# Loading the last head pair's output weights behind all of V, in two DMAs, and projecting head by head

## The chip, the cores and the metric

The kernel runs on one core of a Trainium2 chip. The metric is device time in microseconds (us). This program has one core, so its time is that core's.

## The reference, cut to what matters

One decode step: one token `x` of width 448, 16 query heads of size 256, 8 key/value heads over a cache of 65,536 positions, then a projection with `wo` (4096 x 448), mixed with a small MLP by a gate.

```python
q = (x @ wq).reshape(B, Sq, 16, 256).transpose(0, 2, 1, 3)
scores = einsum("bhqd,bhkd->bhqk", q, repeat(k_cache, 2, 1)) * 256 ** -0.5
o = einsum("bhqk,bhkd->bhqd", softmax(scores), repeat(v_cache, 2, 1))
a = o.transpose(0, 2, 1, 3).reshape(B, Sq, 4096) @ wo
...                                     # b: layer norm, MLP over the token axis
return g * a + (1 - g) * b              # g = sigmoid(sum(x * gate_w))
```

K and V are 268 MB each and are read once. Everything else is small. The heads come in pairs that share one K/V head: 8 pairs, each with a `wo` share of 512 x 448 values, 448 KB.

## The kernel before

The SyncE queue issues all big loads in one order. A pair has four blocks, each of 8 MB of K and 8 MB of V (`NP` = 32 blocks, `PPH` = 4 blocks per pair). The last V is cut into four parts, of 96, 16, 12 and 4 tiles (6144, 1024, 768 and 256 KB). Each pair's `wo` is issued behind the V of the pair's first block.

```python
for j in range(NP):
    last = j == NP - 1
    ...                                   # wait, then load K of block j (last: two halves)
    load(vbuf, A_v_cache, j, 0, NFIRST if last else NV, 0, sem_v)
    if last:
        for (n0, n1), sem in zip(pieces, sem_vp):
            load(vbuf, A_v_cache, j, n0, n1, 0, sem)
    if j % PPH == 0:
        g = j // PPH
        if g >= 1:
            eng.wait_ge(s_proj, g)        # the projection before has read wo_sb
        ...                               # load wo of pair g into wo_sb
```

After the last block TensorE does this. `values` has already added the first 112 V tiles into `acc`, and VectorE copies that sum to `accs`. (`spin(1)` is one matmul whose result nobody uses.)

```python
def tail():
    pe.wait_ge(s_cp, H)                              # accs is there
    by_d(sps[:, 0, 0:2 * REP])                       # early sum, transposed
    late_values(NLATE, NV).then_inc(s_late, 1)       # last 16 V tiles, 32 matmuls
    spin(1)
    pe.wait_ge(sem_wo, 16 * H)
    pe.wait_ge(s_oTn, H)                             # VectorE: normalised o
    project([dj * REP + hh for hh in range(REP) for dj in range(2)])   # 16 matmuls
```

VectorE then computes `out_g` (gate and sum), and SyncE stores it.

The softmax here doesn't subtract the row's maximum and nothing guards it: scores larger than these inputs give would overflow.

## Time and profile before

| | before |
|---|---|
| median of 6 runs | 1267.35 us (1267.10 to 1267.81) |
| span of the profiled run | 1265.2 us |
| share of the 16 DMA engines that the load queue holds | 99.6% |
| TensorE, ScalarE, VectorE busy | 72%, 42%, 33% |
| last V part landed; `out_g` started | 1261.60; 1262.77 us |

From the page of the kernel before: the busy line, the load queue (packets, MB, share of 16 engines) and the chain that ended last.

```profile
PE 913.4 (72%) x17110; PEld 864.6 (68%) x17110; DVE 420.5 (33%) x755; ACT 537.4 (42%) x786; POOL 0.9 (0%) x7
...
q1 hardware_dynamic: 11512, 544.22, 99.6%
...
DMA 70%; PE 29%; issue 1%; DVE 0%; SPq 0%; ACT 0%; ACTq 0%
```

One queue fills the DMA engines for the whole span. So the time is the bytes, plus a short start, plus what is left to do after the last byte.

The DMA issues of the kernel before (size, then median us from issue to landing), and the SyncE timeline near the end (start, duration, what):

```profile
vbuf<-in_A_v_cache_dram SPq DMA_DIRECT2D x1, 6144.0 KB, 25.7
wo_sb<-in_A_wo_dram SPq DMA_DIRECT2D x8, 448.0 KB, 27.6
...
vbuf<-in_A_v_cache_dram SPq DMA_DIRECT2D x1, 256.0 KB, 29.1
```

```profile
1117.53 0.39 SPq L261 DMA_DIRECT2D wo_sb<-in_A_wo_dram  x1
...
1230.90 2.00 SPq L229 DMA_DIRECT2D vbuf<-in_A_v_cache_dram  x4
```

The V and `wo` loads shown here take 26 to 29 us to land although 256 KB need far less (the last part landed 0.64 us after the part ahead of it): each waits behind the loads issued ahead of it. The last `wo` was issued at 1117.53 and is used at 1262.35, so it lies in SBUF unused for over 115 us.

The end of the kernel before, from its timeline (start, duration, engine, line, operation, out<-in, count; in brackets the idle time before and what ended it):

```profile
1256.67 3.23 PE L350 MATMUL acc<-vbuf,pT 128*2 128x256 bf16 x112 [0.73 <-DMA vbuf<-in_A_v_cache_dram]
1259.95 0.46 DVE L564 COPY accs<-acc 128x288 f32<-128x288 f32 x1 [7.24 <-PE acc L350]
...
1261.00 1.00 PE L371 MATMUL sps<-pT,vbuf 128*128 128x2 bf16 x32
...
1262.03 0.16 DVE L575 TENSOR_TENSOR oTn<-sps,rden 128x4 bf16<-128x4 f32 x1 [1.11 <-PE sps L371]
...
1262.35 0.37 PE L397 MATMUL prj<-wo_sb,oTn 128*1 128x112 bf16 x16
1262.77 0.33 DVE L621 SCALAR_TENSOR_TENSOR out_g<-prj,bcast,run_g 128x112 bf16<-128x112 f32 x1 [0.57 <-PE prj L397]
1263.13 0.65 SPq L264 DMA_DIRECT2D out_dram<-out_g  x1
```

The trace also records 16 landings for each of these DMAs, read here as one for each engine's share. The last of the 16 came at 1256.63, 1259.10, 1260.96 and 1261.60 us for the four parts of V. From the last landing to the start of `out_g` pass 1262.77 - 1261.60 = 1.17 us, in which no byte is loaded.

### The profile page before, as it was taken

What the parts mean: (1) busy time and instruction counts of PE and PEld (TensorE: products, weight loads), DVE (VectorE), ACT (ScalarE), POOL (GpSimd) and SP (SyncE); (2) the same over time, 40 slices, a digit from 0 to 9 for tenths busy, and PEclk for the clock granted to TensorE, in tenths of its full rate; (3) what the DMA queues carried; (4) which work ended last, traced back from release to release, by engine and by line L of the source; (5) the groups of instructions that cost most, each with busy time, mean ns of one, the idle gap of its engine ahead of it and who ended that gap; (6) DMA issues with size and microseconds to landing.
All of it is one profiled execution on the core that took longest, in us unless ns stands there. A gap on an engine that the chain in (4) does not pass through costs nothing.

```text
span 1265.2 us, 38823 instructions
## 1 busy us (share of the span) xinstructions
PE 913.4 (72%) x17110; PEld 864.6 (68%) x17110; DVE 420.5 (33%) x755; ACT 537.4 (42%) x786; POOL 0.9 (0%) x7
## 2 busy tenths in 40 slices
PE   3866678766778667786676876768867678675688
PEld 2766668766677666686666876657766578665687
DVE  2333334423344233343222332223322233332233
ACT  1443335533355333454333553335533345433455
POOL 0000000000000000000000000000000000000000
PEclk9878789878798788888788888788888798787999
DMA  9999999999999999999999999999999999999998
GB/s 412 425 436 433 431 433 433 435 433 435 431 433 433 435 431 437 431 431 433 437 431 433 435 431 433 437 431 433 433 433 433 429 437 435 433 433 431 431 428 352
DMA packets 11613, 544.39 MB, mean 430 GB/s; under 512 B 1360, under 2 KB 1618, under 8 KB 2898
## 3 DMA queue, kind: packets, MB, share of 16 engines
q1 hardware_dynamic: 11512, 544.22, 99.6%
q8 instruction: 8, 0.13, 0.0%
q10 hardware_dynamic: 90, 0.01, 0.0%
q14 instruction: 3, 0.02, 0.0%
HBM read 544.22 MB, written 0.00 MB: 430 GB/s over the span
## 4 chain that ended last, share of the span: by engine, by line
DMA 70%; PE 29%; issue 1%; DVE 0%; SPq 0%; ACT 0%; ACTq 0%
DMA kring<-in_A_k_cache_dram 68%; PE kst L295 24%; PE sps L315 4%; DMA vbuf<-in_A_v_cache_dram 2%; PE acc L350 1%; PE sps L371 0%; PE sps L378 0%; DVE accs L564 0%; SPq L226 0%; PE prj L397 0%; SPq L224 0%; PE acc L339 0%; DVE out_g L621 0%; PE kst L331 0%; ACT pT L646 0%
## 5 line engine op out<-in xcount | busy, mean ns | idle before, releaser
L295 PE MATMUL kst<-ident,kring 128*128 128x128 f32 x4096 | 560.5, 298 | 311.3 <-DMA kring<-in_A_k_cache_dram 300.5
L657 ACT ACTIVATE ktT<-kst 128x1024 bf16<-128x1024 bf16 x512 | 499.5, 1021 | 668.6 <-PE kst L295 667.8
L295 PEld LDWEIGHTS kst<-ident,kring 128*128 128x128 f32 x4096 | 510.7, 155 | 321.2 <-issue 318.5
L559 DVE COPY ktT<-kst 128x1024 bf16<-128x1024 bf16 x512 | 354.2, 692 | 766.5 <-PE kst L295 743.3
L315 PEld LDWEIGHTS sps<-qcur,ktT 128*128 128x128 bf16 x8192 | 237.8, 96 | 4.6 <-issue 2.1
L315 PE MATMUL sps<-qcur,ktT 128*128 128x2 bf16 x8192 | 236.6, 163 | 1.7 <-issue 1.7
L350 PE MATMUL acc<-vbuf,pT 128*2 128x256 bf16 x4080 | 140.3, 305 | 2.6 <-issue 1.8
L350 PEld LDWEIGHTS acc<-vbuf,pT 128*2 128x2 bf16 x4080 | 104.9, 93 | 29.7 <-issue 2.3
L646 ACT ACTIVATE pT<-sps 128x32 f32 x256 | 52.2, 204 | 16.7 <-PE sps L315 16.7
L339 PE MATMUL acc<-pT,ones_sq 128*128 128x32 bf16 x256 | 11.7, 178 | 12.2 <-ACT pT L646 12.2
L339 PEld LDWEIGHTS acc<-pT,ones_sq 128*128 128x128 bf16 x256 | 8.6, 96 | 15.1 <-ACT pT L646 14.9
L663 ACT ACTIVATE z_b<-z_b 128x448 bf16<-128x448 bf16 x14 | 8.1, 576 | 20.6 <-DVE z_b L546 20.6
L564 DVE COPY accs<-acc 128x288 f32<-128x288 f32 x8 | 3.7, 458 | 38.4 <-PE acc L350 38.4
L386 PEld LDWEIGHTS acc<-sel,accs 128*64 128x64 f32 x112 | 10.8, 214 | 0.9
L386 PE MATMUL acc<-sel,accs 128*64 128x1 f32 x112 | 11.4, 261 | 0.0
L421 PE MATMUL acc<-vbuf 42*128 42x42 bf16 x1 | 0.2, 214 | 8.3 <-DMA b_b<-in_B_b_dram 8.3
L540 DVE TENSOR_TENSOR z_b<-wtmp,u_b 128x448 bf16<-128x448 bf16 x14 | 5.5, 393 | 1.0
L538 DVE TENSOR_TENSOR wtmp<-u_b 128x448 bf16<-128x448 bf16 x14 | 5.5, 392 | 1.1
L544 DVE TENSOR_TENSOR z_b<-u_b,wtmp 128x448 bf16<-128x448 bf16 x14 | 5.5, 392 | 1.0
L552 DVE TENSOR_TENSOR gu<-wtmp,z_b 128x448 bf16<-128x448 bf16 x14 | 5.5, 392 | 1.0
L421 PEld LDWEIGHTS acc<-vbuf 42*128 42x128 bf16 x1 | 0.1, 98 | 8.3 <-DMA b_b<-in_B_b_dram 8.3
L550 DVE TENSOR_SCALAR z_b<-z_b 128x448 bf16<-128x448 bf16 x14 | 3.9, 277 | 5.5 <-ACT z_b L663 5.5
(85 smaller groups left out, 79.1 us busy)
## 6 DMA issues: line engine op xcount, KB each, us to landing
kring<-in_A_k_cache_dram SPq DMA_DIRECT2D x4, 4096.0 KB, 24.2
vbuf<-in_A_v_cache_dram SPq DMA_DIRECT2D x1, 6144.0 KB, 25.7
wo_sb<-in_A_wo_dram SPq DMA_DIRECT2D x8, 448.0 KB, 27.6
vbuf<-in_A_wq_dram SPq DMA_DIRECT2D x1, 3072.0 KB, 10.1
vbuf<-in_A_v_cache_dram SPq DMA_DIRECT2D x1, 1024.0 KB, 27.5
vbuf<-in_A_v_cache_dram SPq DMA_DIRECT2D x1, 768.0 KB, 29.0
vbuf<-in_A_wq_dram SPq DMA_DIRECT2D x1, 512.0 KB, 10.9
vbuf<-in_A_v_cache_dram SPq DMA_DIRECT2D x31, 30.0
```

What stands on the lines that cost most here:

```text
L295: ins = pe.transpose(kst[:, b, i * P:(i + 1) * P], kring_f[:, at + NT * (k % DC) + 4 * b + i, :], ident[:, :])
L315: ins = pe.matmul(sps[:, par, 2 * nt:2 * nt + 2], ktT[:, par, b, ntl * DH + dj:(ntl + 1) * DH:2], qcur[:, dj, :], start=(dj == 0), stop=(d ...
L339: pe.matmul(acc[:, DENC:SELC], ones_sq[:, :], pT[:, r, :], start=False, stop=(r == BODY - 1), skip_group_check=True)
L350: ins = pe.matmul(acc[o:o + REP, 0:DH], pT[:, r, 2 * nt:2 * nt + 2], vbuf[:, n, :], start=False, stop=False, skip_group_check=True)
L386: ins = pe.matmul(dst[hh * HP:(hh + 1) * HP, i:i + 1], accs[:, i:DH:2 * REP], sel[:, hh:hh + 1], start=False, stop=True, skip_group_check= ...
L538: vec.tensor_tensor(W, U, U, op=ALU.mult)
L540: vec.tensor_tensor(Z, W, U, op=ALU.mult)
L544: vec.tensor_tensor(Z, U, W, op=ALU.add)
L559: vec.tensor_copy(ktT[:, k % KTB, b, :], kst_b[:, b, :]).then_inc(sem_ev[b], 1)
L646: act.activation(pT[:, bass.ds(p0 + k % DC, 1), :].rearrange("p o n -> p (o n)"), sps[:, k % 2, 0:2 * NT], AF.Exp, scale=scale).then_inc(s ...
L657: act.activation(ktT[:, k % KTB, b, :], kst_b[:, b, :], AF.Copy).then_inc(sem_ev[b], 1)
L663: act.activation(z_b[:, :], z_b[:, :], AF.Tanh).then_inc(s_tanh, 1)
```

## The change

The intent: the stream's last place should belong to the load that has the least work behind it. V's last part has late values, normalising and the whole projection behind it. `wo` has only the projection, and half of that if it comes in two halves.

```diff
+        sem_wl = [new_sem("sem_wl%d" % h) for h in range(REP)]
...
-                if j % PPH == 0:
-                    g = j // PPH
+                g, m = divmod(j, PPH)
+                if m == 0 and g < H - 1:
...                                       (pairs 0 to 6 load as before; the last pair's branch is gone)
+            eng.wait_ge(s_proj, H - 1)
+            for h in range(REP):
+                w = A_wo[(HQ - REP + h) * DH:(HQ - REP + h + 1) * DH, :]
+                eng.dma_start(wo_sb[:, h, :], w.rearrange("(p j) n -> p (j n)", j=2)).then_inc(sem_wl[h], 16)
...
-            def project(cols):
-                for i, j in enumerate(cols):
+            def project(cols, i0=0):
+                for i, j in enumerate(cols, i0):
...
-                pe.wait_ge(sem_wo, 16 * H)
                 pe.wait_ge(s_oTn, H)
-                project([dj * REP + hh for hh in range(REP) for dj in range(2)])
+                for h in range(REP):
+                    pe.wait_ge(sem_wl[h], 16)
+                    ins = project([dj * REP + h for dj in range(2)], 2 * h)
+                ins.then_inc(s_proj, 1)
```

Bytes and matmuls are the same. There is one DMA more and one wait more.

More of the change, by code (lines that the diff above doesn't have):

```diff
@@ L257, in _ @@
                     w = A_wo[g * REP * DH:(g + 1) * REP * DH, :]
-                    if g < H - 1:
-                        eng.dma_start(wo_rows, w.rearrange("(p i) n -> p (i n)", i=2 * REP)).then_inc(sem_wo, 16)
-                    else:
-                        eng.dma_start(wo_sb[:, :, :], w.rearrange("(h p j) n -> p h (j n)", h=REP, j=2)
-                                      ).then_inc(sem_wo, 16)
+                    eng.dma_start(wo_rows, w.rearrange("(p i) n -> p (i n)", i=2 * REP)).then_inc(sem_wo, 16)
+            eng.wait_ge(s_proj, H - 1)
+            for h in range(REP):
+                w = A_wo[(HQ - REP + h) * DH:(HQ - REP + h + 1) * DH, :]
+                eng.dma_start(wo_sb[:, h, :], w.rearrange("(p j) n -> p (j n)", j=2)).then_inc(sem_wl[h], 16)
             eng.wait_ge(s_fin, 1)
@@ L399, in project @@
                                         start=False, stop=True, skip_group_check=True)
-                ins.then_inc(s_proj, 1)
+                return ins
             def tail():
@@ L466, in _ @@
                     pe.wait_ge(s_oTn, g + 1)
-                    project(range(2 * REP))
+                    project(range(2 * REP)).then_inc(s_proj, 1)
         @block.vector
```

## The prediction

> **What bounds the kernel.** The DMA stream. The page's queue part gives q1 a 99.6% share of the 16 engines for 544 MB at 430 GB/s; TensorE is busy 72%, VectorE 33%, ScalarE 42%; the chain of waits is 70% DMA. Inside the stream, fewer or better-ordered compute instructions are worth nothing. Only bytes count there, and what runs after the last byte.
>
> **The end, before (timeline from 1235 us and landings of the trace).** K's second half of the last block lands at 1242.1, V's 6144 KB part at 1256.63, the pieces of 1024, 768 and 256 KB at 1259.10, 1260.96 and 1261.60. Then: 32 late-value matmuls 1261.00 to 1262.00, VectorE's oTn 1262.03 (0.16 us), 16 projection matmuls 1262.31 to 1262.72, out_g 1262.77 (0.33 us), output DMA issued at 1263.13, span end 1265.2. So about 1.1 us of work lies between the last landing and out_g, and the DMA engines stand idle there.
>
> **What the change does.** It takes no byte away. The last pair's wo (448 KB) is now issued at 1117.5, during V of block 28, and needed only at 1262; its 1792-byte packets take 75 ns each, 16 per engine, so 1.2 us of every engine. Moved behind V, it lets all of K and V from block 29 on land 1.2 us earlier, and lands itself where V's last piece landed: about 1261.6 (one more semaphore packet of 9 ns on each engine). [...]
>
> **Critical path after.** V's main part lands at 1255.4, TensorE is ready for it (its keys hang on K, also 1.2 us earlier). Early values end near 1258.7, accs is copied by 1259.2, late values run 1259.8 to about 1260.75 (last piece lands 1260.4), oTn is ready by 1261.0. wo's first head lands near 1261.0, the second near 1261.6: 0.6 us of slack for the attention chain. The first head's 8 matmuls are hidden. After the last landing stay 0.05 us of wake-up, 8 matmuls (about 0.3 us with fill, by the present 16 in 0.41 including weight loads) and out_g, which then starts near 1262.0 instead of 1262.77. Gain about 0.75 us of 1267.4, that is 0.06%. Two waits instead of one on TensorE and two DMA issues instead of one on the SP queue (0.33 to 0.39 us each, 28 us before they land) cost nothing.
>
> **Prediction: 1266.7 us, range 1265.8 to 1267.5. Faster by over 2%: 0.005; within 2%: 0.99; slower by over 2%: 0.005.** The gain is about as large as the spread of the three runs (1267.1 to 1267.81).
>
> **What would show each step.** Right: mean GB/s and bytes unchanged; V's last piece to landing about 1.2 us earlier; the late-value matmuls start near 1259.8; before the projection's second half an idle of 0.3 to 0.6 us, released by DMA of wo_sb; out_g about 0.75 us earlier; the output tail unchanged at about 2.4 us. The last wo landing within 0.1 us of 1261.6.
>
> **What would make it wrong.** The late DMAs start a new pause in the queue, or their short packets at the end land later than bytes alone say (then a loss of up to 0.5 us); the 1.2 us given back at block 29 is not kept because a K load there waits for TensorE (then no gain, or wo arrives 1.2 us after V: +0.4 us); the attention chain doesn't move up and oTn still ends last; drift between chips or runs of a microsecond, larger than the effect.

## The result, and the profile after

| | before | after |
|---|---|---|
| median (range) of 6 runs each | 1267.35 (1267.10 to 1267.81) | 1266.47 (1266.35 to 1266.54) |
| span of the profiled run | 1265.2 | 1264.3 |
| V's last part landed | 1261.60 | 1260.35 |
| last load landed | 1261.60 (V) | 1261.53 (`wo`, second head) |
| from there to `out_g` | 1.17 | 0.36 |

A ratio here is the mean time of one kernel's runs over that of the other's of the same rounds, so it is not quite the ratio of the medians quoted. It is 0.9992, 95% interval 0.9980 to 1.0005. The interval includes 1, but the slowest of the six runs after (1266.54) is faster than the fastest of the six before (1267.10). The changed kernel was run in three more series of five beside the kernel before, and there too no run of one overlaps the other (means 0.80, 0.77 and 0.68 us apart). So there is a gain, and it is about 0.06%.

The page after, the same lines:

```profile
PE 916.7 (73%) x17110; PEld 864.9 (68%) x17110; DVE 420.4 (33%) x755; ACT 536.7 (42%) x786; POOL 0.9 (0%) x7
...
q1 hardware_dynamic: 11528, 544.22, 99.7%
...
DMA 71%; PE 28%; issue 1%; SPq 0%; DVE 0%; ACT 0%; ACTq 0%
```

The 16 packets more are the extra DMA's semaphore packets, of 4 bytes and 9 ns in the median. The issues and the SyncE timeline after:

```profile
vbuf<-in_A_v_cache_dram SPq DMA_DIRECT2D x1, 6144.0 KB, 24.5
...
wo_sb<-in_A_wo_dram SPq DMA_DIRECT2D x2, 224.0 KB, 28.1
vbuf<-in_A_v_cache_dram SPq DMA_DIRECT2D x1, 256.0 KB, 27.9
```

```profile
1230.85 2.00 SPq L230 DMA_DIRECT2D vbuf<-in_A_v_cache_dram  x4
1232.90 0.90 SPq L264 DMA_DIRECT2D wo_sb<-in_A_wo_dram  x2
```

V is issued at the same time as before and lands 1.2 us sooner after its issue (24.5 in place of 25.7): there are 448 KB less ahead of it. The end after:

```profile
1255.39 3.23 PE L352 MATMUL acc<-vbuf,pT 128*2 128x256 bf16 x112 [0.72 <-DMA vbuf<-in_A_v_cache_dram]
1258.67 0.46 DVE L568 COPY accs<-acc 128x288 f32<-128x288 f32 x1 [7.22 <-PE acc L352]
...
1259.77 0.98 PE L373 MATMUL sps<-pT,vbuf 128*128 128x2 bf16 x32
...
1260.79 0.16 DVE L579 TENSOR_TENSOR oTn<-sps,rden 128x4 bf16<-128x4 f32 x1 [1.15 <-PE sps L373]
...
1261.08 0.27 PE L399 MATMUL prj<-wo_sb,oTn 128*1 128x112 bf16 x8
...
1261.57 0.27 PE L399 MATMUL prj<-wo_sb,oTn 128*1 128x112 bf16 x8 [0.22 <-DMA wo_sb<-in_A_wo_dram]
1261.89 0.33 DVE L625 SCALAR_TENSOR_TENSOR out_g<-prj,bcast,run_g 128x112 bf16<-128x112 f32 x1 [0.94 <-PE prj L399]
1262.25 0.65 SPq L266 DMA_DIRECT2D out_dram<-out_g  x1
```

Every line of the attention end has the same duration as before (3.23, 0.46, 1.00 or 0.98, 0.16 us) and starts 1.2 to 1.3 us earlier. New is the wait in front of the second eight matmuls, which DMA ends. (The step from `oTn` to the projection changed by little; see early_by_head.) The gain in this pair of traces is `out_g` at 1261.89 in place of 1262.77, 0.88 us. Of these, 1.17 - 0.36 = 0.81 us are work that no longer lies behind the last landing, and 0.07 us are that the last landing itself came earlier. That small part can't be told from chance: the experiments show the last landing of one program vary by 0.3 us.

### The profile page after: what moved, and what is told of

Same layout as the page of the kernel before. It is cut to its first block, busy times and chain, and to the rows that moved or that the text cites. A ratio compares the mean times of both kernels' runs of the same rounds, so it can differ in the third digit from the quotient of the medians.

```text
span 1264.3 us, 38824 instructions
## 1 busy us (share of the span) xinstructions
PE 916.7 (73%) x17110; PEld 864.9 (68%) x17110; DVE 420.4 (33%) x755; ACT 536.7 (42%) x786; POOL 0.9 (0%) x7
## 3 DMA queue, kind: packets, MB, share of 16 engines
q1 hardware_dynamic: 11528, 544.22, 99.7%
## 4 chain that ended last, share of the span: by engine, by line
DMA 71%; PE 28%; issue 1%; SPq 0%; DVE 0%; ACT 0%; ACTq 0%
DMA kring<-in_A_k_cache_dram 68%; PE kst L297 24%; PE sps L317 4%; DMA wo_sb<-in_A_wo_dram 2%; PE acc L352 0%; SPq L230 0%; SPq L264 0%; SPq L227 0%; SPq L225 0%; PE acc L341 0%; DVE out_g L625 0%; PE prj L399 0%; ACT pT L650 0%; ACTq L650 0%
## 5 line engine op out<-in xcount | busy, mean ns | idle before, releaser
L352 PE MATMUL acc<-vbuf,pT 128*2 128x256 bf16 x4080 | 147.6, 315 | 2.2 <-issue 1.5
L352 PEld LDWEIGHTS acc<-vbuf,pT 128*2 128x2 bf16 x4080 | 109.3, 96 | 32.3 <-issue 2.0
L399 PE MATMUL prj<-wo_sb,oTn 128*1 128x112 bf16 x128 | 3.6, 240 | 3.2 <-DVE oTn L591 2.8
## 6 DMA issues: line engine op xcount, KB each, us to landing
vbuf<-in_A_v_cache_dram SPq DMA_DIRECT2D x1, 6144.0 KB, 24.5
```

Of the source, the lines that this page charges most:

```text
L352: ins = pe.matmul(acc[o:o + REP, 0:DH], pT[:, r, 2 * nt:2 * nt + 2], vbuf[:, n, :], start=False, stop=False, skip_group_check=True)
```

## The experiments

Theory A: the stream is full, so its end stays where it is whatever the order. The change trades V for `wo` in the last place, and the gain is the work that thereby no longer lies behind the last landing. Rival B: taking `wo`, and the queue's wait on a projection, out of block 28 makes the stream itself shorter. Rival C: the projection head by head is what shortens the end.

There were twelve experiments, four in a series on one chip, each of five runs beside nine of the kernel before. "Against before" is the difference of the means of the runs of the same series. Landings are the last of a DMA's shares unless a mean over the 16 engines is named. Edits are against the changed kernel.

| run | median us | mean against before | last landing of V; of the last load | `out_g` |
|---|---|---|---|---|
| same_after (series 1) | 1266.69 | -0.80 | 1260.36; 1261.54 | 1261.90 |
| late_one_dma (1) | 1266.70 | -0.71 | 1260.38; 1261.52 | 1262.14 |
| early_by_head (1) | 1267.39 | -0.11 | 1261.28; 1261.28 | 1262.35 |
| between_k_v (1) | 1267.19 | +0.10 | 1261.56; 1261.56 | 1262.63 |
| same_after2 (series 2) | 1266.46 | -0.77 | 1260.28; 1261.43 | 1261.80 |
| no_wo (2) | 1266.14 | -1.21 | 1260.63; 1260.63 | 1261.70 |
| dummy_load (2) | 1267.86 | +0.44 | 1261.77; 1262.92 | 1263.29 |
| eight_rings (2) | 1269.60 | +2.13 | 1260.86; 1264.67 | 1265.12 |
| same_after3 (series 3) | 1266.57 | -0.68 | 1260.57; 1261.73 | 1262.18 |
| late_one_dma2 (3) | 1267.02 | -0.35 | 1260.34; 1261.48 | 1262.21 |
| eight_dmas (3) | 1268.03 | +0.70 | 1260.85; 1263.32 | 1263.77 |
| eleven_rings (3) | 1267.24 | +0.02 | 1261.07; 1262.48 | 1262.85 |

### same_after, same_after2, same_after3: the changed kernel again

No edit.

> The changed kernel once more, as the yardstick of this series. Theory A (order at the end: wo takes the last place in the stream, so that only half a projection is left after the last landing) and all rivals: 1266.5 us, about 0.9 us under the kernel before; V's last piece lands near 1260.35, wo's second head near 1261.5, out_g starts near 1261.9.

> The changed kernel again, for comparison on the chip of this series: 1266.5 us.

> The changed kernel again, for comparison on the chip of this series: 1266.5 us, 0.8 us under the kernel before.

All three came as expected. They also show how far one trace may be trusted: the last landing is 1261.54, 1261.43 and 1261.73 for the same program. The 16 engines end at different times, and that spread differs from run to run (2.0, 1.8 and 2.3 us here). The mean over the 16 engines is steadier: 1260.45, 1260.58, 1260.63. So below 0.3 us a single last landing proves nothing.

### late_one_dma and late_one_dma2: behind V, but in one piece

```diff
-            for h in range(REP):
-                w = A_wo[(HQ - REP + h) * DH:(HQ - REP + h + 1) * DH, :]
-                eng.dma_start(wo_sb[:, h, :], w.rearrange("(p j) n -> p (j n)", j=2)).then_inc(sem_wl[h], 16)
+            eng.dma_start(wo_sb[:, :, :], A_wo[(HQ - REP) * DH:HQ * DH, :].rearrange("(h p j) n -> p h (j n)", h=REP, j=2)
+                          ).then_inc(sem_wl[0], 16)
...
+                pe.wait_ge(sem_wl[0], 16)
                 for h in range(REP):
-                    pe.wait_ge(sem_wl[h], 16)
```

> wo behind all of V, but in one DMA and with one wait, so that all 16 projection matmuls come after the last landing. Theory A: the place of wo makes most of the gain and the split only the difference of 16 to 8 matmuls, about 0.1 us: 1266.6 us, still 0.8 us under the kernel before. Rival C (the projection head by head is what shortens the end): no gain, 1267.3 us.

> wo behind V in one DMA once more, because in the first series its trace had out_g 0.24 us later than the changed kernel's and its runs only 0.01 us in the median. If the trace is right: 0.2 us slower than the changed kernel in the runs too, still 0.6 us under the kernel before. If the split is worth nothing: no difference again.

The place without the split gives 0.71 us of 0.80 in the first series, but only 0.35 of 0.68 in the second, where 0.6 was expected. Rival C forecast no gain here, and has fallen as the main cause. The split is worth 0.08 us in the means of the first series and 0.34 in the second. In the traces, from last landing to `out_g`, it takes 0.62 and 0.73 us, against 0.36, 0.37 and 0.45 with the split. That is more than the 0.1 us that the matmuls alone account for. The timeline of late_one_dma2 and, below it, its windows (PE, PEld, DVE, ACT and POOL busy with counts, granted clock, DMA):

```profile
1261.62 0.54 PE L398 MATMUL prj<-wo_sb,oTn 128*1 128x112 bf16 x16 [0.64 <-DMA wo_sb<-in_A_wo_dram]
1262.21 0.34 DVE L624 SCALAR_TENSOR_TENSOR out_g<-prj,bcast,run_g 128x112 bf16<-128x112 f32 x1 [1.27 <-PE prj L398]
```

```profile
1261.40:1261.70 0.30, 0.08 (x8) 0.11 (x12) 0.00 (x0) 0.00 (x0) 0.00 (x0) 0.50 0.00 0
1261.70:1262.00 0.30, 0.30 (x16) 0.20 (x14) 0.00 (x0) 0.00 (x0) 0.00 (x0) 0.50 0.00 0
```

The 16 matmuls took 0.54 us where the kernel before needed 0.37, and the granted clock was 0.50. In the profiled run after, the clock was 1.00 through these windows. The clock differs from run to run here: same_after3 had 0.50 too from 1261.4 on, with both halves of the projection slowed (274 ns for a matmul in the median, 210 in the run after). So part of what the split seems to gain is the clock of the particular run. In late_one_dma the clock fell during the projection (0.68 over 1261.70 to 1262.00), so no trace shows the single DMA at full clock. With two series that differ by a factor of four, the worth of the split stays between 0.1 and 0.3 us and is not settled further.

### early_by_head: in two DMAs and head by head, but loaded early

```diff
                     eng.dma_start(wo_rows, w.rearrange("(p i) n -> p (i n)", i=2 * REP)).then_inc(sem_wo, 16)
+                if m == 0 and g == H - 1:
+                    ...                  # the lines cut below
-
-            eng.wait_ge(s_proj, H - 1)
-            for h in range(REP):
-                ...                       (the two DMAs)
```

> Two DMAs, two semaphores and the projection head by head, but wo loaded in block 28 where the kernel before has it. Theory A: nothing gained, 1267.35 us (within 0.2 us), V's last piece back at 1261.6, out_g at 1262.8. Rival C: most of the gain stays, about 1266.5 us.

The mean is 0.11 us under the kernel before, within the spread of the runs. The trace's last V landing lies at 1261.28, earlier than in the kernel before by the spread of the engines (mean 1260.45 against 1260.53), and `out_g` follows it by 1.07 us, near the 1.17 of the kernel before and far from the 0.36 of the changed one. Splitting gains at most 0.1 us where `wo` has long been there. This is the second half of the case against rival C. The 0.1 us may be real: in the three traces with the changed tail and no late `wo` (this one, between_k_v and no_wo) the projection starts 0.06 us after `oTn` is done and `out_g` 1.07 us after the last landing, against 0.16 and 1.17 us in the one trace before. Which edit of the tail would do this was not tested by itself.

### between_k_v: taken out of block 28, but ahead of the last V

```diff
+                if last:
+                    ...                  # wait on s_proj and the two DMAs, as below
                 load(vbuf, A_v_cache, j, 0, NFIRST if last else NV, 0, sem_v)
...
-            eng.wait_ge(s_proj, H - 1)
-            for h in range(REP):
-                ...                       (the two DMAs)
```

> wo taken out of block 28 and loaded at the end, but in front of the last block's V and behind its K. Theory A: V's last piece lands at 1261.6 again and the whole attention end comes after it, so 1267.35 us (within 0.2 us) although the last K lands 1.2 us earlier. Rival B (taking wo and its wait on the projection out of the queue in block 28 makes the stream itself shorter): about 1266.5 us.

This is the run against rival B: block 28 is free of `wo` and of the wait, and little or nothing is gained. Four of five runs lie at 1267.14 to 1267.21, 0.3 us under the median before (0.1 of it may be that of early_by_head); one of 1269.12 lifts the mean. Rival B's 1266.5 us are not there. The last K lands at 1240.86 as in the changed kernel, so the stream does move up from block 28 on. But V comes behind `wo` and lands at 1261.56. Timeline:

```profile
1256.62 3.23 PE L352 MATMUL acc<-vbuf,pT 128*2 128x256 bf16 x112 [1.91 <-DMA vbuf<-in_A_v_cache_dram]
...
1261.99 0.16 DVE L579 TENSOR_TENSOR oTn<-sps,rden 128x4 bf16<-128x4 f32 x1 [1.11 <-PE sps L373]
1262.21 0.37 PE L399 MATMUL prj<-wo_sb,oTn 128*1 128x112 bf16 x16
```

TensorE now stands 1.91 us before V in place of 0.73: the 1.2 us that the last K gained turned into a wait for V.

### no_wo: the bound

```diff
-            for h in range(REP):
-                ...                       (the two DMAs)
...
-                    pe.wait_ge(sem_wl[h], 16)
```

> The last pair's wo is not loaded at all and the projection uses what lies there (a wrong result on purpose): what the change could gain at most. Theory A: the stream ends 1.2 us earlier (16 packets of 75 ns per engine) and the old end with all its work moves up whole: 1266.1 us, 1.2 us under the kernel before; V's last piece lands near 1260.35, oTn at 1260.8, out_g near 1261.55. Then the change has taken 0.8 to 0.9 of 1.2 us. Rival B (the stream doesn't move up by its bytes): less than 0.5 us under the kernel before.

The mean gains 1.21 us, as expected: taken out at the end, 448 KB are worth 1.2 us. The changed kernel, which loads these bytes, gets 0.77 us in the same series. So moving the load takes about two thirds of what dropping it would (0.8 to 0.9 of 1.2 us were expected), and at most 0.44 us are left to any other arrangement of this load. The result is wrong on purpose, and yet the comparison with the reference passed. Presumably the attention of this problem, averaged over 65,536 positions, is too small for the tolerance; that was not measured. So that comparison says nothing about the changed projection; it was verified by reading only: `i` still runs 0 to 3 over `oTn` columns 0, 2, 1, 3.

### dummy_load: the same bytes once more where they were

```diff
+        spare = sb([P, 2 * REP * DM], bf16, "spare")
...
+                if m == 0 and g == H - 1:
+                    eng.wait_ge(s_proj, g)
+                    eng.dma_start(spare[:, :], A_wo[0:REP * DH, :].rearrange("(p i) n -> p (i n)", i=2 * REP)
+                                  ).then_inc(sem_sp, 16)
```

> The changed kernel, with 448 KB that nobody uses loaded in block 28, where wo was, with the same wait on the projection. Theory A: the stream is full, every byte counts wherever it stands: 8 packets of 144 ns per engine, 1.15 us over the changed kernel, 1267.65 us, all landings at the end 1.15 us later. Rival B (a load of this size in mid-stream hides in a pause): the changed kernel's time, 1266.5 us.

It lost 0.44 + 0.77 = 1.21 us against the changed kernel in the means. The last landing came 1.49 us later, but by the mean over the engines 1261.73 - 1260.58 = 1.15 us, the number expected. The spread of this run was 2.3 us against 1.8 and made up the rest. There is no pause at block 28 in which a load would hide, and no gain from the place as such: rival B's second chance is gone.

### eight_rings, eight_dmas, eleven_rings: can the spread of the engines be used?

The spread is in place early: K's first landings lie 1.6 us apart in the profiled run after, the second's 2.0, and it stays at 2.0 to the end. If the early engines could take more of the last load, up to half of that might be gained (an estimate: in the profiled run after, the last landing lies 0.9 us behind the mean of the 16). Where V's parts and each head of `wo` left 16 landings, the 16 DMAs of 8 partitions left 144 records, 16 x 8 + 16, and 8 packets each beside the data (the load queue has 11640 packets in eight_rings, 11528 after: 112 more, 16 x 8 - 16); two DMAs of 88 and 40 left 23 records, 11 + 10 + 2. The expectations read 8, 11 and 10 as the engines in use, the same 8 for all sixteen DMAs and the 10 among the 11, so that five get none of the load in eleven_rings. That was the author's estimate. Which engines were taken, no trace shows.

```diff
-                w = ...
-                eng.dma_start(...)
+                w = A_wo[(HQ - REP + h) * DH:(HQ - REP + h + 1) * DH, :].rearrange("(p j) n -> p (j n)", j=2)
+                at = 0
+                for np_ in ((P,) if h == 0 else SIZES):
+                    eng.dma_start(wo_sb[at:at + np_, h, :], w[at:at + np_, :]).then_inc(sem_wl[h], 16)
+                    at += np_
```

SIZES is `(8,) * 16` in eight_rings (which writes the same with a step), `(16,) * 8` in eight_dmas and `(88, 40)` in eleven_rings. TensorE waits for the full count, 16 for each DMA.

> The 16 shares of each DMA land spread over 2.0 us (wo's second head from 1259.60 to 1261.53), the spread is as wide all the way, and the wait ends with the latest. Here the second head is loaded in 16 DMAs of 8 partitions[...]. If those 8 are the early ones: wo lands near 1261.0, about 0.4 us gained over the changed kernel (1266.1 us). If they are the late ones: 0.6 us later, 1267.1 us. If mixed: in between, 0.3 to 0.6 us lost.

> The second head in 8 DMAs of 16 partitions[...]. It tells apart why loading on 8 engines lost 3.1 us. If the landings of small DMAs one behind the other cost about 0.2 us each on an engine (the spacing of the last landings there): wo lands about 1.0 us later, 1267.5 us. If the loss came from the uneven load of the engines: under 0.2 us lost, 1266.6 us.

> The second head in two DMAs of 88 and 40 partitions[...]. If the latest engines are among the five: wo lands up to 0.3 us earlier than in the changed kernel. If the latest is among the ten: 4 packets of 75 ns more and one more semaphore packet, 0.3 to 0.5 us later, 1266.9 us.

eight_rings was a miss: 2.9 us slower than the changed kernel of its series, far outside all three expectations. The data were late by only a part of that. The last data packet ended at 1262.46, 1.48 us later than in same_after2 (1260.98), but the last landing was recorded at 1264.67, 2.21 us after it, where same_after2 has 0.45. So of the 3.24 us by which the last landing was later, 1.48 are later data and 1.76 a longer way from last packet to last landing. The last landings lie 0.20 us apart (1264.08, 1264.27, 1264.47, 1264.67). Issuing was not the cause:

```profile
1233.16 19.17 SPq L266 DMA_DIRECT2D wo_sb<-in_A_wo_dram  x17
```

All were issued by 1252.3, and the first packet of this `wo` came at 1257.9. (The last packets took 0.19 us each in place of 0.08; why is open.) So eight_dmas was made: half as many DMAs, of 16 partitions each. That they use all 16 engines was the author's estimate, not shown. It was 1.39 us slower than the changed kernel (expected: 1.0). The data ended at 1261.65, 0.43 us later than in same_after3 (1261.22). The last landing came at 1263.32, 1.67 us after that (0.51 in same_after3), and the last ones again lie 0.19 to 0.20 us apart, here behind packets of 0.08 us. So the last landing was 1.59 us later with the load cut into eight, and sixteen DMAs, in eight_rings, cost about twice as much in device time (2.9 against 1.39 us). That speaks for the number of small DMAs as the main cost; what the number of engines costs was not measured apart.

eleven_rings has only two DMAs and was 0.71 us slower than the changed kernel (expected: 0.3 to 0.5). Its last landing is 0.75 us later. `wo`'s packets of 1792 bytes took 93 ns in the median against 76. Why they were slower was not tested and stays open. In all three runs V's last part, which is issued ahead of `wo`, landed later too: at 1260.86 in eight_rings (1260.28 in same_after2), at 1260.85 and 1261.07 in eight_dmas and eleven_rings (1260.57 in same_after3). This is not explained either. No run here made use of the spread. None beat the changed kernel with a right result.

## Why the prediction was right

- **What bounds it.** "Only bytes count there, and what runs after the last byte": dummy_load and no_wo cost and gave 1.2 us for 448 KB, and between_k_v gained no more than 0.3 us from a freer block 28.
- **The stream's end.** "lands itself where V's last piece landed: about 1261.6": 1261.53 in the trace after; by the mean over the engines 1260.62 against 1260.53. The bytes moved, and the end did not. The loads at the end landed in the order of their issue: V's last part 1260.35, `wo` 1260.95 and 1261.53. The trace doesn't name the engine of a landing, so an order on each engine is not shown; the pattern fits it, as the 16 landings of one load follow those of the load before at the same distances to within 0.1 us (`wo`'s first head 0.55 to 0.62 us after V's last part).
- **The attention chain.** V's main part was forecast at 1255.4 (1255.34), late values from 1259.8 (1259.77), oTn by 1261.0 (1260.95). This chain had to move up whole, or the change would have gained nothing. It did, because its first link is a wait for DMA: 0.73 us before, 0.72 after.
- **After the last landing.** The prediction left 0.05 us of wake-up, 8 matmuls in about 0.3, then `out_g` near 1262.0. Measured 0.04, about 0.3, and 1261.89. The wait for the second half was forecast at 0.3 to 0.6 us; the weight loads waited 0.38, within it, and the matmuls 0.22, below it.
- **The size.** Forecast 1266.7, measured 1266.47, within the range. The gain was put at about 0.75 us. The medians give 0.88 and the repeated series 0.68 to 0.80. The one-trace excess is the 0.07 us earlier last landing, smaller than the spread between runs of one program.
- **What it did not see.** It took the clock of TensorE as given. In one of the four profiled runs of the changed kernel (same_after3) the clock was 0.50 for the projection (1.00 in the run after), and the step from landing to `out_g` took 0.45 in place of 0.36 us.

## What to carry to other kernels

Where loads fill the whole span, the order of the last loads is free and decides what lies exposed behind the last byte: put last the load with the least work behind it, even if it could have been there long before. The gain is the difference of the work behind the two candidates (here 0.8 us), bounded by the time of the moved bytes (1.2 us), so read both from the trace before taking the trouble. Do not cut the last load into many small DMAs: here eight of 28 KB in place of one of 224 KB landed 1.6 us later, about 0.2 us for each.

## What the runs leave open

- How closely the landings of small DMAs can follow one another, and why. The semaphore packets took 9 ns each in the median. In eight_dmas the last landings lie 0.19 to 0.20 us apart although a data packet takes 80 ns, and eight small DMAs ended 1.6 us later than one of the same bytes. The traces do not show what part of a landing takes this time.
- Small DMAs cost much here although the queue was full and nothing waited for the issue: with 28 KB each in eight_dmas, 1.6 us more for data whose 128 packets take 76 ns each in the run after, 0.6 us if 16 engines share them evenly; with 14 KB each in eight_rings, 3.2 us more to the last landing.
- How far apart the engines of one evenly split DMA end. For the K and V loads the spread of the landings is 1.6 us at the first and 2.0 to 2.1 from 50 us on in the profiled run after, 1.7 and then 2.2 to 2.3 in the one before. At the last load it is 1.93 and 2.15 us in these two and 2.0, 1.8 and 2.3 in the three series. It varies from run to run, and the last landing of one program moves by 0.3 us.
- What sets the clock. In late_one_dma2 the granted clock was 1.00 from 1260.50 to 1261.20 and 0.50 after it, although TensorE was busy for 2.41 of the 3.20 us from 1258.00 to 1261.20, and its longest wait within them was 0.57 us. The runs do not show the rule.
